# Sixteen more items of a top-k attention turned by VectorE squares and a round trip through DRAM, on one core

## The chip, the cores and the metric

The kernel runs on one core of one Trainium2 chip. The metric is the device time of one execution in microseconds (us). The kernel before was run three times: 1480.83 us is the median, 1480.33 and 1480.93 us are the ends.

## The reference

Two blocks follow each other, all in float32. First comes attention that keeps only the 32 largest scores of each query:

```
B, H, S, D = 8, 8, 576, 64
scores = scale * np.matmul(q, k.transpose(0, 1, 3, 2))
kth = np.partition(scores, -32, axis=-1)[..., -32:-31]
scores = np.where(scores >= kth, scores, -1e9)
attn = softmax(scores, axis=-1)
x = np.matmul(attn, v)            # to (B*S, H*D) = (4608, 512)
```

Then an MLP with the exact GELU:

```
h = x @ w_in                      # 512 -> 2048
out = gelu(h) @ w_out             # 2048 -> 512
```

## The kernel before

**Items and slots.** Two heads make a pair, and 128 query rows of a pair make an item; the last 64 rows of four heads make an item of their own kind. A batch has 18 items (16 main, 2 of the last rows), the eight batches have 144. Everything is done in a written-out order of slots, one for each item (the loop `for n in range(ahead)`). Two batches, 36 slots, make a round, and everything repeats from round to round. An item is called here by its place in the round, its number modulo 36 (`i % RINGS`).

**What a slot holds.** An item passes through several slots. Slot n makes the scores of item n + 2 on TensorE, and in an even slot those of item n + 3 too (`scores`); an ACT copy brings each from PSUM into one of six SBUF buffers named `s`. The keys are 512 (main) and 64 (the end of each head); the products with the end keys are made apart (`last_keys`). VectorE then looks for the 32 largest of item n by four rounds of MAX8 and MATCH_REPLACE8 (`top_k`); before them stand the larger halves of item n + 1 (`larger`) and, in some slots, transposes that lay out q and k of a later pair (`squares` in `transpose_qk`). At the end of `top_k` the callback `last` takes the reciprocal of the sums of item n - 1 (`inverse`, L504), which GpSimd has finished in `add_small` (tile `den`, L510), and which come from the exponentials of item n - 1 on ScalarE (`softmax`, L529). GpSimd then makes the threshold of item n (`threshold`, L497 and L498, which `select` on ScalarE waits for), normalises item n - 1 (`normalise`, L552), and adds up halves for item n + 2 (`sum_up`).

**How the attention weights are turned.** The product with v needs the normalised weights with the keys on the partitions. There are two ways:

- Items that are not "squared": in slot i + 2 TensorE makes nine 128x128 transposes (`tails`, L619, and `both`, L649), and ScalarE copies them from PSUM into the tile `pt` (L629, L664).
- Items for which `squared(i)` is true, which are even ones only: in slot i + 2 VectorE transposes all 32x32 squares of the item's buffer in place (`square_p`, the callback `middle` of `top_k`, L569, ahead of the third round); four DMAs write it to DRAM (`write_p`, L579); in slot i + 3 four DMAs read it back with the squares in their new places (`read_p`, L586). All are issued from SyncE's queue, in the order in which the program has them.

An even and an odd item share a `pt` tile, of which there is one. In slot i + 3 of the odd item the product with v is made for both (`attend`, L715), right after the scores, and copied to `xT`, from which the MLP takes its tokens.

**The MLP's pieces.** The MLP is cut into pieces, and each slot issues some of them between its other work; `room_in(n)` says how many. Several PSUM tiles are shared: the first of two scores of an even slot and the MLP's `h_ps` take turns in one tile.

**Loads.** From batch 1 on, q and k of a pair are loaded by eight DMAs each (L124): four for the 512 main rows and four for the 64 end rows of two heads and two halves of their 64 columns.

Of the kernel before, what the change touches and what calls it, by code (L numbers as in the profile page):

```python
# [8 lines left out]
TOPK = 32  # L9
# [5 lines left out]
def kernel(  # L15
# [26 lines left out]
    P = 128  # L42
# [68 lines left out]
    def load(n, pair, queue=None, queue2=None):  # L111
        if pair >= n_pairs:
            return
        queue = queue or nc.sync
        queue2 = queue2 or queue
        b, h0 = pair // NP, 2 * (pair % NP)
        src = sources[n]
        if n != "v" and pair >= SQUARES:
            t = flat[n][0]
            for e in range(2):  # L120
                for d in range(2):
                    rows, cols = slice((2 * e + d) * SQ, (2 * e + d + 1) * SQ), slice(d * SQ, (d + 1) * SQ)
                    for at, lo, hi, by in ((0, 0, SM, queue), (SM + e * TL, SM, S, queue2)):
                        by.dma_start(  # L124
                            out=t[rows, at : at + hi - lo].rearrange("i (c j) -> i c j", j=SQ),
                            in_=src[b, h0 + e, lo:hi, cols].rearrange("(c i) j -> i c j", i=SQ),
                        )
            return
        t = raw_of(n, pair)
        for e in range(2):  # L130
            queue.dma_start(
                out=t[:, 0:NM, e, :], in_=src[b, h0 + e, 0:SM].rearrange("(t p) d -> p t d", p=P)
            )
            queue2.dma_start(out=t[e * TL : (e + 1) * TL, NM, e, :], in_=src[b, h0 + e, SM:S])
# [141 lines left out]
    def transpose_qk(pair, first=False):  # L276
# [4 lines left out]
        def squares(c):  # L281
            rq, rk, kt = flat["q"][0], flat["k"][0], kt_of.get(pair)
            if c == 0:
                nc.vector.transpose(kt[:, 0:q_tail], rk)
            elif c == 1:
                nc.vector.transpose(kt[:, q_tail:], rq[:, SM:])
            else:
                nc.vector.transpose(q_of[pair], rq[:, 0:SM])
# [15 lines left out]
        def piece(c):  # L304
            if c == 0:
                kt_of[pair] = work.tile([P, 2 * P + SM], f32, tag="kt", bufs=NP + 2, name="kt")
            if c == 2:
                q_of[pair] = work.tile([P, SM], f32, tag="qm", bufs=NP, name="qm")
            (squares if pair >= SQUARES else by_pe)(c)
            done.add(c)  # L310
            ahead = 1 if pair >= SQUARES else 2
            if pair + ahead >= SQUARES > pair:
                return
            if c != 0 and done >= {1, 2}:
                load("q", pair + ahead)
            if (c == 0 if pair >= SQUARES else c != 0 and done >= {0, 1, 2}):
                load("k", pair + ahead)
# [5 lines left out]
    S_of, stat_of = {}, {}  # L323

# [19 lines left out]
    def last_keys(i, t_ps):  # L344
# [3 lines left out]
        if t < NM:  # L348
            nc.tensor.matmul(
                t_ps[:, 0:P], lhsT=q_of[pair][:, t * P : (t + 1) * P],  # L350
                rhs=kt_of[pair][:, SM : SM + P], start=True, stop=True,
# [8 lines left out]
        for r in range(2):  # L360
            kt = kt_of[pair + r]
            for e in range(2):
                nc.tensor.matmul(
                    t_ps[half(r, e), r * TL : (r + 1) * TL],
                    lhsT=kt[:, SM + P + e * TL : SM + P + (e + 1) * TL],
                    rhs=kt[:, SM + e * TL : SM + (e + 1) * TL],
                    start=True, stop=True,
                )
# [5 lines left out]
    def scores(i, second=False):  # L374
# [7 lines left out]
        if t < NM:  # L382
            q_t, kt = q_of[pair][:, t * P : (t + 1) * P], kt_of[pair]
            for e in range(2):
                rows = slice(e * D, (e + 1) * D)
                nc.tensor.matmul(  # L386
                    s_ps[:, e], lhsT=q_t[rows, :], rhs=kt[rows, 0:SM], start=True, stop=True
# [7 lines left out]
        else:  # L395

            for r in range(2):
                kt = kt_of[pair + r]
                for e in range(2):
                    rows = slice(e * D, (e + 1) * D)  # L400
                    nc.tensor.matmul(
                        s_ps[half(r, e), r, :], lhsT=kt[rows, SM + P + e * TL : SM + P + (e + 1) * TL],
                        rhs=kt[rows, 0:SM], start=True, stop=True,
# [53 lines left out]
    def top_k(i, last, middle):  # L457
# [21 lines left out]
        for r, (src, dst, x) in enumerate(rounds):  # L479
            if 16 * r == TOPK:  # L480
                middle()
            for e in range(2):
                nc.vector.max(x[:, e], src[:, e])  # L483
# [96 lines left out]

    def read_p(i):

        if squared(i):
            d = turned.pop(i)
            for k in range(P // SQ):
                nc.sync.dma_start(  # L586
                    out=pt_now[0][k * SQ : (k + 1) * SQ, :, 0:P], in_=d[:, :, k, :]
                )

    def transposes(i):  # L590
# [3 lines left out]
        if squared(i):  # L594

            def keys_only(ahead):
                pt_now[0] = work.tile([P, 2 * NM + 1, 2 * P], f32, tag="pt", bufs=1, name="pt")
# [7 lines left out]
        def tails(ahead):  # L605
# [3 lines left out]
            if t % 2 == 0:  # L609
                pt_now[0] = work.tile([P, 2 * NM + 1, 2 * P], f32, tag="pt", bufs=1, name="pt")  # L610
# [480 lines left out]
    def room_in(n):  # L1091
# [6 lines left out]
        return sizes[x] + (1 if x % 2 == 0 else -1)  # L1098
# [55 lines left out]
    for n in range(ahead):  # L1154
# [23 lines left out]
        product = attend(n - 3)  # L1178
# [71 lines left out]
        run_gelus()  # L1250
        if n < N:
            top_k(n, lambda: inverse(n - 1), lambda: square_p(n - 2))
# [26 lines left out]
        if n == 5:  # L1279
            load("q", SQUARES)  # L1280
# [39 lines left out]
```

## Time and profile before

| | |
|---|---|
| median of three runs | 1480.83 us |
| the profiled execution | 1479.73 us |
| its span | 1478.0 us |
| instructions | 27006 |
| TensorE busy (PE) | 1461.6 us, 99% |
| weight loads (PEld) | 1147.9 us, 78% |
| VectorE (DVE) | 1294.3 us, 88% |
| GpSimd (POOL) | 1140.1 us, 77% |
| ScalarE (ACT) | 1099.9 us, 74% |
| DMA | 112.94 MB, of 16 engines' time 35.3% in SyncE's queue |

An engine's busy time is the time in which one of its instructions runs, waits left out. Rows of the timeline begin with the start and the duration in us, then the engine and the line of the kernel. "SPq" is SyncE's queue as it issues DMAs; such a row's duration is that of the issuing, not of the transfer. A wait is shown in brackets with what ended it. Two records of TensorE stand for each float32 matmul, one for each transpose. A bracket `x8` says that eight records are merged in the row.

### The profile page before, as it was taken

The numbers are of one execution on the slowest core, as the hardware profiler recorded it, in microseconds if no ns is written. First come the engines' busy times: TensorE is split into PE (matmuls) and PEld (weight loads), VectorE is DVE, ScalarE is ACT, GpSimd is POOL, SyncE is SP. The second block draws the span as 40 slices with busy tenths as digits, with TensorE's granted clock in tenths as the row PEclk, the third lists the DMA queues.
The fourth block names the chain that finished last, engine by engine and source line by source line (L and its number), as shares of the span: only waits on it lengthen the run. The fifth ranks groups of instructions, "written<-read, shape, count | busy, mean of one in ns | idle before, by whom it ended". The sixth has DMA issues, their size and how long they took to land. (4 is left out here: it accounts for less than half of the span.)

```text
span 1478.0 us, 27006 instructions
## 1 busy us (share of the span) xinstructions
PE 1461.6 (99%) x8817; PEld 1147.9 (78%) x8817; DVE 1294.3 (88%) x3318; ACT 1099.9 (74%) x1942; POOL 1140.1 (77%) x1291
## 2 busy tenths in 40 slices
PE   8999999999999999999999999999999999999999
PEld 6876677877777777887777778787777777787787
DVE  8999899999999988999999987999999997998701
ACT  7999977877777687777777778777777777776620
POOL 6877567877898879877898978886788887987732
PEclk9999999999999999999999999999999999999999
DMA  7424310045435322345534331345453421233300
GB/s 198 143 86 124 84 48 1 24 88 101 95 73 93 66 58 52 65 95 108 105 83 81 69 61 47 66 93 99 97 103 73 89 55 41 61 61 72 70 15 15
DMA packets 477645, 112.94 MB, mean 76 GB/s; under 512 B 413216, under 2 KB 469056, under 8 KB 477504
## 3 DMA queue, kind: packets, MB, share of 16 engines
q1 hardware_dynamic: 476240, 110.78, 35.3%
q8 instruction: 70, 1.15, 0.3%
q14 instruction: 71, 0.58, 0.1%
q10 hardware_dynamic: 1200, 0.39, 0.1%
q0 software_dynamic: 64, 0.03, 0.0%
HBM read 73.39 MB, written 37.75 MB: 75 GB/s over the span
## 5 line engine op out<-in xcount | busy, mean ns | idle before, releaser
L773 PE MATMUL h_ps<-xT,w_in_sb 128*128 128x256 f32 (+1 forms) x2560 | 536.2, 361 | 0.1
L773 PEld LDWEIGHTS h_ps<-xT,w_in_sb 128*128 128x128 f32 x2560 | 436.5, 190 | 73.4 <-issue 25.2
L483 DVE MAX8 top<-lists 128x8 f32<-128x576 f32 (+1 forms) x792 | 476.4, 641 | 0.0
L486 DVE MATCH_REPLACE8 lists<-top,lists 128x288 f32<-128x288 f32 (+1 forms) x528 | 307.9, 589 | 0.0
L552 POOL TENSOR_TENSOR s<-s,rden 128x1152 f32<-128x1152 f32 x135 | 285.8, 2117 | 0.3 <-DVE rden L504 0.3
L529 ACT ACTIVATE s<-s,bias 128x576 f32<-128x576 f32 x288 | 225.4, 787 | 11.0 <-issue 0.4
L517 ACT ACTIVATE s<-s,neg 128x576 f32<-128x576 f32 x288 | 225.5, 793 | 1.7 <-POOL neg L497 1.6
L510 POOL TENSOR_SCALAR den<-den 128x2 f32<-128x2 f32 x144 | 31.4, 218 | 215.9 <-ACT s L529 210.2
L455 POOL TENSOR_TENSOR lists<-lists 128x576 int32<-128x576 int32 x132 | 186.2, 1410 | 4.0
L447 POOL TENSOR_TENSOR lists<-s 128x576 int32<-128x576 int32 x133 | 187.2, 1407 | 0.0
L715 PE MATMUL o<-pt,raw_v 128*64 128x256 f32 x1280 | 153.0, 384 | 1.8 <-ACT s L529 1.1
L715 PEld LDWEIGHTS o<-pt,raw_v 128*64 128x64 f32 x1280 | 87.8, 136 | 85.8 <-issue 37.2
L789 ACT ACTIVATE g<-h_ps 128x512 f32<-128x512 f32 x144 | 78.2, 594 | 100.6 <-PE h_ps L773 100.4
L929 PE MATMUL y_ps<-w_out_sb,sum 128*128 128x256 f32 x472 | 140.4, 379 | 0.0
L394 ACT ACTIVATE s<-s_ps 128x1024 f32<-128x1024 f32 x127 | 125.5, 1035 | 10.5 <-PE s_ps L386 10.3
L664 ACT COPY pt<-tp 128x1024 f32<-128x1024 f32 x85 | 86.6, 1019 | 62.2 <-PE tp L649 62.1
L386 PE MATMUL s_ps<-kt,qm 64*128 64x512 f32 x512 | 129.4, 618 | 0.8 <-ACT s L392 0.8
L504 DVE RECIPROCAL rden<-den 128x2 f32<-128x2 f32 x144 | 23.2, 161 | 108.6 <-POOL den L510 107.4
L486 DVE MATCH_REPLACE8 lists<-first,lists 128x288 f32<-128x288 f32 x264 | 114.3, 439 | 0.0
L929 PE MATMUL y_ps<-w_out_sb,g 128*128 128x256 f32 x480 | 113.4, 379 | 0.0
L483 DVE MAX8 first<-lists 128x8 f32<-128x288 f32 x268 | 106.6, 436 | 0.0
L929 PEld LDWEIGHTS y_ps<-w_out_sb,g 128*128 128x128 f32 x480 | 91.2, 190 | 12.4
(167 smaller groups left out, 2533.1 us busy)
## 6 DMA issues: line engine op xcount, KB each, us to landing
turned<-s SPq DMA_DIRECT2D x192, 144.0 KB, 3.5
pt<-turned SPq DMA_DIRECT2D x192, 144.0 KB, 3.2
raw_v<-in_v_dram SPq DMA_DIRECT2D x64, 128.0 KB, 2.4
out_dram<-y SPq DMA_DIRECT2D x30, 256.0 KB, 2.1
raw_q<-in_q_dram SPq DMA_DIRECT2D x112, 64.0 KB, 2.0
raw_k<-in_k_dram SPq DMA_DIRECT2D x112, 64.0 KB, 2.0
w_out_sb<-in_moe_w_in_dram SPq DMA_DIRECT2D x14, 511.8 KB, 4.8
w_out_sb<-in_moe_w_out_dram SPq DMA_DIRECT2D x10, 511.8 KB, 4.1
```

What stands on the lines that cost most here:

```text
L386: nc.tensor.matmul(s_ps[:, e], lhsT=q_t[rows, :], rhs=kt[rows, 0:SM], start=True, stop=True)
L394: nc.scalar.activation(spread(s, S + TL, SM), s_ps, func=AF.Copy, scale=scale)
L447: nc.gpsimd.tensor_tensor(t[:, :, 1].bitcast(i32), a.bitcast(i32), b.bitcast(i32), op=ALU.add)
L455: nc.gpsimd.tensor_tensor(into_of(i)[:, :, 1].bitcast(i32), both, top, op=ALU.subtract)
L483: nc.vector.max(x[:, e], src[:, e])
L486: nc.vector.match_replace(dst[:, e], x[:, e], src[:, e], LOWEST)
L517: nc.scalar.activation(s, s, func=AF.Prelu, bias=st["neg"][:, e : e + 1], scale=1.0, alpha=STEEP)
L529: nc.scalar.activation(s, s, func=AF.Exp, bias=st["bias"][:, e : e + 1], scale=1.0, accum_out=st["den"][:, e : e + 1],)
L552: nc.gpsimd.tensor_tensor(s, s, wide, op=ALU.mult)
L715: nc.tensor.matmul(o[e * D : (e + 1) * D, 0:n], lhsT=vt[:, j, e, :], rhs=pt[:, e * NJ + j if j < NM else NM, :], start=(j == 0), stop=(j = ...
L773: nc.tensor.matmul(h_tile(u)[:, i, :], lhsT=w_in_sb[:, ko, f * P : (f + 1) * P], rhs=xT[:, ko, c0 : c0 + n], start=(ko == 0), stop=(ko == ...
L929: nc.tensor.matmul(acc[names][:, k], lhsT=lhsT, rhs=rhs, start=(j == 0 and k == 0), stop=(j == FT // 2 - 1 and k == 1),)
```

## The change

Sixteen odd items (places 3, 13, 21, 25 and 29 of a round, from item 29 on) are squared too. For such an item i, which `later(i)` tells:

- the nine transposes on TensorE and their ACT copies go; VectorE squares, four writes and four reads come;
- in slot i + 1 the reciprocal is taken between the last two MAX8 instead of behind them (`early`), and normalising comes ahead of the next item's threshold on GpSimd;
- in slot i + 2 the squares are made behind the first round of `top_k` instead of ahead of the third (`late`), and the writes come as soon as they are done; loads that the slot issues come after them;
- in slot i + 3 the product with v moves from the slot's beginning to its end, and two MLP pieces move from slot i + 2 to slot i + 3 (`moved`).

Beside that, q and k of all pairs from batch 1 on are loaded by four DMAs each instead of eight. For it the first head's 64 end keys are taken from the beginning of its rows and its main keys from behind them, v's rows are loaded in the same order, the end keys of a pair lie at both ends of its tile (`both_ends`), and the transpose that lays out q's end rows is 64 instead of 128 columns wide.

```diff
             for e in range(2):
+                at = e * TL if n == "k" else 0
                 for d in range(2):
...
-                    for at, lo, hi, by in ((0, 0, SM, queue), (SM + e * TL, SM, S, queue2)):
-                        by.dma_start(
-                            out=t[rows, at : at + hi - lo].rearrange("i (c j) -> i c j", j=SQ),
-                            in_=src[b, h0 + e, lo:hi, cols].rearrange("(c i) j -> i c j", i=SQ),
-                        )
+                    queue.dma_start(
+                        out=t[rows, at : at + S].rearrange("i (c j) -> i c j", j=SQ),
+                        in_=src[b, h0 + e, :, cols].rearrange("(c i) j -> i c j", i=SQ),
+                    )
...
-                nc.vector.transpose(kt[:, q_tail:], rq[:, SM:])
+                nc.vector.transpose(kt[:, q_tail : q_tail + TL], rq[:, SM:S])
...
             if c != 0 and done >= {1, 2}:
-                load("q", pair + ahead)
+                issue(lambda: load("q", pair + ahead))
             if (c == 0 if pair >= SQUARES else c != 0 and done >= {0, 1, 2}):
-                load("k", pair + ahead)
+                issue(lambda: load("k", pair + ahead))
...
+    def both_ends(pair):
+        kt = kt_of[pair]
+        return spread(kt, SM + TL, TL) if pair >= SQUARES else kt[:, SM : SM + P]
...
-    def top_k(i, last, middle):
+    def top_k(i, last, middle, early, late):
...
-            if 16 * r == TOPK:
+            if 16 * r == TOPK and not late:
                 middle()
             for e in range(2):
                 nc.vector.max(x[:, e], src[:, e])
+                if early and e == 0 and r == len(rounds) - 1:
+                    last()
+            if r == 0 and late:
+                middle()
...
-            if r == len(rounds) - 1:
+            if r == len(rounds) - 1 and not early:
                 last()
...
     def squared(i):
-        return SINGLE.stop - 2 < i < N - 2 and i % 2 == 0 and items[i][1] < NM and i % RINGS != 12
+        if not SINGLE.stop - 2 < i < N - 2 or items[i][1] == NM:
+            return False
+        if i % 2 == 0:
+            return i % RINGS != 12
+        return i % RINGS in LATER
+    def later(i):
+        return i % 2 == 1 and squared(i)
     RINGS = 2 * len(items) // B
+    LATER = (3, 13, 21, 25, 29)
...
                 nc.sync.dma_start(
-                    out=pt_now[0][k * SQ : (k + 1) * SQ, :, 0:P], in_=d[:, :, k, :]
+                    out=pt_now[0][k * SQ : (k + 1) * SQ, :, i % 2 * P : (i % 2 + 1) * P], in_=d[:, :, k, :]
                 )
...
-        return sizes[x] + (1 if x % 2 == 0 else -1)
+        moved = 2 * (later(n - 3) - later(n - 2))
+        return sizes[x] + (1 if x % 2 == 0 else -1) + moved
...
-        product = attend(n - 3)
+        product = not later(n - 3) and attend(n - 3)
...
         run_gelus()
         mlp(left[0])
         run_gelus()
+        if later(n - 3):
+            attend(n - 3)
+            copy_x()
         if n < N:
-            top_k(n, lambda: inverse(n - 1), lambda: square_p(n - 2))
+            top_k(
+                n, lambda: inverse(n - 1), lambda: square_p(n - 2), later(n - 1), later(n - 2)
+            )
             write_p(n - 2)
             flush()
...
+        if later(n - 1):
+            normalise(n - 1)
         threshold(n)
...
-        normalise(n - 1)
+        if not later(n - 1):
+            normalise(n - 1)
         sum_up(n + 2)
```

More of the change, by code (lines that the diff above doesn't have):

```diff
@@ L130, in load @@
         for e in range(2):
+            end = TL if pair >= SQUARES and e == 0 else S
+            main = end % S
             queue.dma_start(
-                out=t[:, 0:NM, e, :], in_=src[b, h0 + e, 0:SM].rearrange("(t p) d -> p t d", p=P)
+                out=t[:, 0:NM, e, :], in_=src[b, h0 + e, main : main + SM].rearrange("(t p) d -> p t d", p=P)
             )
-            queue2.dma_start(out=t[e * TL : (e + 1) * TL, NM, e, :], in_=src[b, h0 + e, SM:S])
+            queue2.dma_start(out=t[e * TL : (e + 1) * TL, NM, e, :], in_=src[b, h0 + e, end - TL : end])
     load("k", 0, nc.scalar, nc.gpsimd)
@@ L350, in last_keys @@
                 t_ps[:, 0:P], lhsT=q_of[pair][:, t * P : (t + 1) * P],
-                rhs=kt_of[pair][:, SM : SM + P], start=True, stop=True,
+                rhs=both_ends(pair), start=True, stop=True,
             )
@@ L386, in scores @@
                 nc.tensor.matmul(
-                    s_ps[:, e], lhsT=q_t[rows, :], rhs=kt[rows, 0:SM], start=True, stop=True
+                    s_ps[:, e], lhsT=q_t[rows, :], rhs=kt[rows, main_keys(pair)], start=True, stop=True
                 )
@@ L401, in scores @@
                     nc.tensor.matmul(
-                        s_ps[half(r, e), r, :], lhsT=kt[rows, SM + P + e * TL : SM + P + (e + 1) * TL],
-                        rhs=kt[rows, 0:SM], start=True, stop=True,
+                        s_ps[half(r, e), r, :], lhsT=kt[rows, end_rows(pair + r, e)],
+                        rhs=kt[rows, main_keys(pair + r)], start=True, stop=True,
                     )
@@ L579, in write_p, with pt_tile @@
                 nc.sync.dma_start(out=d[:, :, rows], in_=s[rows])
+    def pt_tile():
+        return work.tile([P, 2 * NM + 1, 2 * P], f32, tag="pt", bufs=1, name="pt")
     def read_p(i):
@@ L1279 @@
         if n == 5:
+            nc.vector.memset(flat["k"][0][TL:, 0:TL], 0.0)
             load("q", SQUARES)
```

16 lines of the change are left out of this document (12 added, 4 removed).

## The prediction

> **What bounds the kernel now.** I read the page's first part, then a table of three whole rounds of 36 slots, then who waited for whom, then the timeline of the slots that the change touches.
>
> ```profile
> PE 1461.6 (99%) x8817; PEld 1147.9 (78%) x8817; DVE 1294.3 (88%) x3318; ACT 1099.9 (74%) x1942; POOL 1140.1 (77%) x1291
> 355.57:703.63 348.06, 347.65 (x2085) 273.79 (x2083) 321.89 (x833) 262.71 (x470) 286.34 (x323) 1.00 0.40 79
> DVE rden L504 <- POOL den L510: 107.4, 92, 9.7
> ```
>
> TensorE is busy without a break: 347.65 of 348.06 us of a round, 9.67 us a slot. So what it no longer has to do is time won, as long as nothing else is late. Little is spare elsewhere: VectorE works 321.89 us of the round and idles 26.2, nearly all of it at the reciprocal, where it waits for `den` (107.4 us in all).
>
> **TensorE's saving.** One item's transposes, between neighbours in the order:
>
> ```profile
> 1331.42 0.60 PE L891 MATMUL y_ps<-w_out_sb,g 128*128 128x256 f32 x2
> ...
> 1335.10 0.27 PE L619 MATMUL tp_t<-ident,s 128*128 128x128 f32 x1
> 1335.21 0.60 PE L891 MATMUL y_ps<-w_out_sb,g 128*128 128x256 f32 x2
> ...
> 1336.07 1.04 PE L649 MATMUL tp<-ident,s 128*128 128x128 f32 x8
> 1336.94 0.38 PE L891 MATMUL y_ps<-w_out_sb,g 128*128 128x256 f32 x1
> ```
>
> The tail's transpose takes TensorE 1335.21 - 1335.10 = 0.11 us, the eight others 1336.94 - 1336.07 = 0.87 (ends are modelled, so starts count). Sixteen items by 0.98 make 15.7 us, 1.06% of the time. The ACT copies that go with them lie on an engine that is busy 74% and are worth nothing by themselves. The tail behind the last product has the same four MLP blocks in the new order, so nothing is pushed out to the end.
>
> **VectorE.** A square takes 1.36 us (next fence), so 16 add 21.8 us, 6.8 to a round that has 26.2 idle. On average that fits; it is local slots that decide. The narrower layout of q's end rows (0.27 us now) may save up to half of that on 28 transposes, 3.8 us at most and nothing at least; I take 2, hidden in the same idle time. The one new memset is 64x64, below the 0.27 us row in size, and hidden.
>
> **The way over DRAM, on item 129 (place 21).** Its even partner 128 shows what the way costs:
>
> ```profile
> 1269.56 1.36 DVE L569 STREAM_TRANSPOSE s<-s 128x1152 f32<-128x1152 f32 x1
> 1273.60 1.40 DVE L483 MAX8 top<-lists 128x8 f32<-128x576 f32 x2
> 1275.04 0.76 DVE L422 TENSOR_TENSOR lists<-s 128x576 f32<-128x576 f32 x1
> 1275.71 0.81 DVE L483 MAX8 first<-lists 128x8 f32<-128x288 f32 x2
> 1274.30 0.22 POOL L510 TENSOR_SCALAR den<-den 128x2 f32<-128x2 f32 x1
> 1275.99 2.10 POOL L552 TENSOR_TENSOR s<-s,rden 128x1152 f32<-128x1152 f32 x1
> 1270.99 3.38 SPq L579 DMA_DIRECT2D turned<-s  x4
> 1277.10 2.55 SPq L586 DMA_DIRECT2D pt<-turned  x4
> DMA to landing us min/median/max: 2.7/3.3/5.2
> 1283.79 2.38 PE L715 MATMUL o<-pt,raw_v 128*64 128x256 f32 x20
> 1286.10 2.86 PE L773 MATMUL h_ps<-xT,w_in_sb 128*128 128x256 f32 x12
> 1289.01 4.48 PE L773 MATMUL h_ps<-xT,w_in_sb 128*128 128x256 f32 x20
> 1293.33 1.03 PE L927 MATMUL seven<-w_sum,g 128*128 128x256 f32 x4
> ```
>
> From the first write's issue (1270.99) to the first read's (1277.10), which waits for the writes to land, pass 6.1 us; the fourth read goes out 1.9 us later and lands 3.3 us behind its issue (the median). So `pt` is full 11.3 us after the writes begin.
>
> When do the writes of 129 begin? `den` of 129 is ready at 1274.52. The reciprocal now goes between the two last MAX8 (the pair begins at 1273.60, 0.67 us each), at about 1274.55, and normalising, 2.10 us, ends at 1276.85 instead of 1278.09. VectorE does the second MAX8 (0.70), `larger` (0.68) and the first round (0.75), is at the square by 1276.85 too, and is through at 1278.25. But SyncE's queue issues the reads of 128 until 1277.10 + 2.55 = 1279.65, so the writes begin then and `pt` is full at 1290.95.
>
> When does TensorE want it? The product (1286.10 - 1283.79 = 2.31 us) now stands near the slot's end, ahead of two of the four-record MLP steps (20 records take 1293.33 - 1289.01 = 4.32, so 4 take 0.86) and of 1293.33. On an engine that won 0.98 it begins at 1293.33 - 0.86 - 2.31 - 0.98 = 1289.2. It waits 1.75 us there: this item costs 0.8 instead of winning 0.98. The two moved MLP pieces only fill the place that the product left.
>
> **The other four places, by the same steps.**
>
> ```profile
> 1098.24 0.17 DVE L504 RECIPROCAL rden<-den 128x2 f32<-128x2 f32 x1 [1.09 <-POOL den L510]
> 1099.29 2.54 SPq L586 DMA_DIRECT2D pt<-turned  x4
> 1116.71 1.03 PE L927 MATMUL seven<-w_sum,g 128*128 128x256 f32 x4
> 1120.90 0.33 PE L619 MATMUL tp_t<-ident,s 128*128 128x128 f32 x1 [0.35 <-POOL s L552]
> ```
>
> Place 3 (item 111). `den` gates the reciprocal (1.09 us of waiting with both MAX8 done), so it stays at 1098.24; normalised at 1100.55, squared at 1101.95, the reads of 110 are out at 1101.83. `pt` is full at 1113.3, wanted at 1116.71 - 0.86 - 2.31 - 0.98 = 1112.55: 0.7 us of waiting, which would leave 0.3 won. But in the next slot but one TensorE stands at item 113's tail for its normalising (0.35 us), and that chain is not shortened: GpSimd, full here, now normalises before it makes the threshold, and what it did while the reciprocal ran it does behind it, some 0.2 us (the reciprocal's 0.17 and a start). So place 3 costs 0.2.
>
> ```profile
> 1193.21 0.17 DVE L504 RECIPROCAL rden<-den 128x2 f32<-128x2 f32 x1 [0.21 <-POOL den L510]
> 1193.97 0.83 DVE L284 STREAM_TRANSPOSE kt<-raw_k 128x640 f32<-128x640 f32 x1
> 1194.73 0.27 DVE L286 STREAM_TRANSPOSE kt<-raw_q 128x128 f32<-128x128 f32 x1
> 1194.83 3.87 SPq L124 DMA_DIRECT2D raw_k<-in_k_dram  x8
> 1211.92 1.09 PE L401 MATMUL s_ps<-kt 64*64 64x512 f32 x8
> ```
>
> Place 13 (item 121). The reciprocal stays at 1193.21; VectorE passes the second MAX8 (0.70), `larger`, the two layouts above and the first round, and has squared at 1197.8. Behind its writes, ahead of its reads, the order puts k's and q's loads, eight DMAs now: the row has eight in 3.87 us. Writes 3.4, loads 3.9: the reads begin at 1205.1, later than the landing would let them (1203.95). `pt` is full at 1210.3, wanted at 1211.92 - 2.31 - 0.98 = 1208.6. It waits 1.7 and costs 0.7.
>
> ```profile
> 1311.57 0.17 DVE L504 RECIPROCAL rden<-den 128x2 f32<-128x2 f32 x1 [0.24 <-POOL den L510]
> 1313.50 2.55 SPq L586 DMA_DIRECT2D pt<-turned  x4
> 1321.06 0.17 DVE L504 RECIPROCAL rden<-den 128x2 f32<-128x2 f32 x1 [1.40 <-POOL den L510]
> 1332.19 2.10 POOL L552 TENSOR_TENSOR s<-s,rden 128x1152 f32<-128x1152 f32 x1
> ```
>
> Place 25 (item 133). Squared by 1315.3, the reads of 132 are out at 1316.05, `pt` is full at 1327.35, wanted at 1331.42 - 0.90 - 2.31 - 0.98 = 1327.2. That would do. But VectorE has to make up a MAX8 (0.70) behind the wait and a square (1.30 beyond its overlap) where it had 1.40 us of waiting: its next reciprocal comes 0.6 later than 1321.06. GpSimd's slot behind it is full, and item 135 is normalised at 1334.9 instead of 1334.29. TensorE would want it 0.98 ahead of its 1335.10 and waits 0.8. Won: 0.2.
>
> ```profile
> 1000.75 1.42 DVE L483 MAX8 top<-lists 128x8 f32<-128x576 f32 x2
> 999.95 0.22 POOL L510 TENSOR_SCALAR den<-den 128x2 f32<-128x2 f32 x1 [1.93 <-ACT s L529]
> 1004.11 2.54 SPq L586 DMA_DIRECT2D pt<-turned  x4
> 1022.67 1.03 PE L927 MATMUL seven<-w_sum,g 128*128 128x256 f32 x4
> ```
>
> Place 29 (item 101). `den` was ready at 1000.17, so the reciprocal moves up to 1001.42, the square ends at 1005.1, the reads of 100 are out at 1006.65, `pt` is full at 1017.95 and wanted at 1022.67 - 0.86 - 2.31 - 0.98 = 1018.5. Nothing waits: 0.98 won.
>
> **The loads.** A DMA of q or k takes SyncE's queue 0.48 us whatever its size (3.87 / 8), so half as many save 1.9 us of issuing a load, on a queue that nobody waits for in the slots without squares; they buy the room between writes and reads. I cost them at nothing; place 13 has them in its sum.
>
> **Two rules.** The row for transposes is above: 0.98 us of TensorE against 1.36 of VectorE, 5.9 us of issuing and 11.3 us of way. The Trainium skill (VectorE: DVE Perf Modes, Rules for kernel authors) says to turn 128x128 on TensorE where the result may lie in PSUM, or by the DMA's own transposer, and not by a strided plain copy; by it the change would lose. If all sixteen fared as place 21, it would be 16 x 0.8 = 13 us slower. In the other direction, TensorE's row says 99%. The Trainium skill (Perfetto Trace Analysis, Identifying the Most-Contended Engine) says to relieve the most contended engine first, and that matmul busy time is a poor measure of it, to be replaced by the share of weight loads, here 78%. By the first half of that the whole 15.7 us would be won.
>
> **The sum.** Place 29 comes four times: -3.9. Places 25, 21, 13 and 3 come three times: -0.6, +2.4, +2.1, +0.6. Together +0.6 us. Two additions: writes that go out while reads are landing, or next to loads, land later than alone. The slowest landed after 5.2 us, the median after 3.3; I take 0.45 of those 1.9 us, at places 21 and 13: 6 x 0.45 = 2.7. And VectorE comes 0.6 us late out of place 25 into place 29, where slots without waiting follow; I take 0.3 in each of three rounds, 0.9. Total +4.2: 1479.73 + 4.2 = 1483.9 for a profiled execution, and as the median of the runs shown lies 1.1 above it, 1485.0.
>
> **The rivals.**
> 1. *The full way is won.* If the landings are hidden after all (`pt` full two us earlier at places 3, 13 and 21, because the writes need not queue behind the reads, or because TensorE is late there for other reasons), only the chains of places 3 and 25 are left: 4 + 3 + 3 places at 0.98 win 9.8, place 25 0.6, place 3 costs 0.6: 9.8 us faster, 1471; with those chains shortened too, 1465. For it speaks that 0.7 to 1.75 us decide, and that TensorE waits for nothing now; against it, that the queue's order is fixed and that 6.1 us between write and read repeat. It holds from 1.7 us of earlier landing on. 0.34.
> 2. *DMA becomes the bound of the pairs.* Where write, read, write, read follow each other slot by slot, each way lands as late as the slowest does now, 1.9 us more. Then place 21 costs 2.7, 13 2.6, 3 1.6, 25 1.1 and 29 0.3: 3 x 8.0 + 1.2 = 25 us slower, 1506. For it: odd items put a second pair of transfers into a slot. Against: the engines are 40% busy in these rounds (the table's DMA share). 0.14.
> 3. My sum, costs and gains near cancelling: 0.52.
>
> **The numbers.** Less than 0.2%, 3 us, cannot be told from no change here. The likeliest is my sum: 1485.0, with its own range 1480 (no additions, and 2 us from VectorE's narrower transposes) to 1491. Of its 0.52, 0.13 falls within 3 us of now and 0.39 above; rival 1 is faster, rival 2 slower. So faster 0.34, same 0.13, slower 0.53. The range for 8 in 10 takes in rival 1 as worked out but not its last step, and the lower half of rival 2: 1469 to 1497.
>
> **What the profile after would show.** Right: TensorE's busy time lower by about 16 us, its idle time higher by as much or more; waits of the product with v (`o`) for a DMA into `pt`, of 1 to 2 us, at places 13 and 21 and none at 29; the normalising of items 5 and 27 still just ahead of their tails. VectorE about 20 us busier, its wait for `den` well under 107 us. Wrong: no waits of `o` for DMA (then rival 1, and I placed the writes too late); waits of 3 us and more at every place (rival 2); or ACT standing for the writes ahead of its copies of the scores, since the buffer of a squared odd item goes to the item six later in slot i + 3: by my times it would stand until 1285.8 at place 21 and still be in time.

## The result, and the profile after

The changed kernel takes 1523.80 us (median of 4 runs, 1520.12 to 1527.04) against 1480.88: 1.029 times as long, 95% interval 1.0264 to 1.0316. The prediction said 1485.0, within 1469 to 1497. The direction was the likelier one; the size lies far outside, beyond even the rival in which DMA binds (1506).

First the busy times, then the group of `larger`, then who waited for whom (total in us, times, longest), all of the changed kernel. The last two rows are of the kernel before:

```profile
PE 1456.6 (96%) x8673; PEld 1137.4 (75%) x8673; DVE 1335.6 (88%) x3335; ACT 1081.3 (71%) x1910; POOL 1143.4 (75%) x1291
...
L443 DVE TENSOR_TENSOR lists<-s 128x576 f32<-128x576 f32 x133 | 122.8, 924 | 0.6
...
POOL neg L522 <- DVE rden L529: 73.5, 48, 3.6
ACT s L415 <- DMA turned<-s: 34.1, 11, 4.5
ACT s L542 <- POOL neg L522: 27.0, 17, 3.9
PE o L753 <- DMA pt<-turned: 33.2, 18, 4.7
PE h_ps L811 <- ACT s L415: 4.7, 8, 0.7
PE tp_t L657 <- POOL s L577: 4.0, 6, 1.2
...
L422 DVE TENSOR_TENSOR lists<-s 128x576 f32<-128x576 f32 x133 | 100.8, 758 | 0.0
ACT s L517 <- POOL neg L497: 1.6, 6, 0.4
```

TensorE was 99% busy and is 96%: its idle time rose from 16.4 us (1478.0 - 1461.6) to 61.7 (1518.3 - 1456.6), by 45.3. Of these, 29.5 are stands of the product at fourteen of the sixteen new items, 7.7 stands of the product at other pairs, 4.7 stands at `h_ps`, and 2.9 come on top at the tails.

Its busy time fell by 5.0 and not by 16. The transposes are gone as reckoned: counted from start to start, without the stands, the transposes and the products with the end keys beside them take 16.4 us less. But all other matmuls together take 11.4 us more. Some 3 us of these are the ends of records: TensorE stands 50 times where it stood 18 times (stands over 0.15 us), and ahead of a stand the last matmul shows its full length of 0.38 us, where otherwise 0.22 or 0.31 pass until the next one starts. Some 5 us are a slower TensorE after the three longest stands, at place 13 (last section). The rest, some 3 us, was not followed up. Together 45.3 + 11.4 - 16.4 = 40.3, what the span grew by.

VectorE got 41.3 us busier (1294.3 to 1335.6). The squares account for 21.8 of that; another 22.0 are the row of `larger` (L443): 122.8 us, where the kernel before had 100.8 for the same 133 instructions (L422). The narrower layouts of q's end rows give 1.8 back.

The slot of item 129, which the prediction followed, on all engines (VectorE, GpSimd, SyncE's queue, ScalarE, TensorE). The last two rows are the two reciprocals of the same slot in the kernel before:

```profile
1312.11 0.17 DVE L529 RECIPROCAL rden<-den 128x2 f32<-128x2 f32 x1 [0.22 <-POOL den L535]
1312.96 2.11 DVE L443 TENSOR_TENSOR lists<-s 128x576 f32<-128x576 f32 x1
1315.73 1.36 DVE L603 STREAM_TRANSPOSE s<-s 128x1152 f32<-128x1152 f32 x1
...
1323.52 0.14 DVE L529 RECIPROCAL rden<-den 128x2 f32<-128x2 f32 x1
1312.36 2.11 POOL L577 TENSOR_TENSOR s<-s,rden 128x1152 f32<-128x1152 f32 x1 [0.28 <-DVE rden L529]
1314.43 0.72 POOL L522 TENSOR_SCALAR neg<-top 128x2 f32<-128x2 f32 x1
1314.65 2.55 SPq L625 DMA_DIRECT2D pt<-turned  x4
1317.30 3.32 SPq L613 DMA_DIRECT2D turned<-s  x4
1324.55 2.54 SPq L625 DMA_DIRECT2D pt<-turned  x4
1315.19 0.78 ACT L542 ACTIVATE s<-s,neg 128x576 f32<-128x576 f32 x1 [1.97 <-POOL neg L522]
1319.83 1.00 ACT L415 ACTIVATE s<-s_ps 128x1024 f32<-128x1024 f32 x1
1324.73 1.03 ACT L415 ACTIVATE s<-s_ps 128x1024 f32<-128x1024 f32 x1 [3.90 <-DMA turned<-s]
1327.29 0.26 ACT L379 ACTIVATE s<-t_ps 128x128 f32<-128x128 f32 x1
1320.89 1.13 PE L811 MATMUL h_ps<-xT,w_in_sb 128*128 128x256 f32 x4 [0.67 <-ACT s L415]
1329.72 2.38 PE L753 MATMUL o<-pt,raw_v 128*64 128x256 f32 x20 [2.30 <-DMA pt<-turned]
...
1274.93 0.14 DVE L504 RECIPROCAL rden<-den 128x2 f32<-128x2 f32 x1
1283.17 0.17 DVE L504 RECIPROCAL rden<-den 128x2 f32<-128x2 f32 x1
```

Five things are to be seen.
- `larger` (1312.96) lies beside the normalising that was moved ahead (GpSimd, 1312.36 to 1314.47). It takes 2.11 us instead of 0.76 and ends 0.6 us behind it, as if it had run only once GpSimd was through. So the square ends at 1317.09, 4.98 us behind the reciprocal. The prediction had 3.7.
- VectorE goes from this reciprocal to the next (1323.52) without a gap, in 11.41 us. In the kernel before the same slot took 8.24 (1283.17 - 1274.93).
- The writes (1317.30) go out 0.21 us behind the square and 0.10 behind the partner's four reads (1314.65 + 2.55 = 1317.20), which stand ahead of them on the queue. The odd item's own reads follow 7.25 us after the writes, and TensorE stands 2.30 us for them.
- ScalarE's second copy of the scores (1324.73) stands 3.90 us until those writes have landed, for it fills the buffer that they read. The copy of the keys' rows (1327.29) comes behind it. That copy empties the one PSUM bank which the product, too, writes. Here it was in time: the product waited longer, for its reads.
- `h_ps` stood 0.67 us for the first of the two copies (1319.83). That one did not stand for the writes. It came late because ScalarE had stood 1.97 us for `neg`, GpSimd's threshold, which comes behind the normalising that was moved ahead. In the trace each of the eight stands of `h_ps` follows such a stand of ScalarE, of 0.5 to 2.0 us. In all, ScalarE stands 27.0 us for `neg`; before, it was 1.6.

### The profile page after: what moved, and what is told of

Read it like the earlier page. It is cut to its first block, busy times and chain, and to the rows that moved or that the text cites. A ratio compares the mean times of both kernels' runs of the same rounds, so it can differ in the third digit from the quotient of the medians.

```text
span 1518.3 us, 26593 instructions
## 1 busy us (share of the span) xinstructions
PE 1456.6 (96%) x8673; PEld 1137.4 (75%) x8673; DVE 1335.6 (88%) x3335; ACT 1081.3 (71%) x1910; POOL 1143.4 (75%) x1291
## 5 line engine op out<-in xcount | busy, mean ns | idle before, releaser
L753 PE MATMUL o<-pt,raw_v 128*64 128x256 f32 x1280 | 157.2, 391 | 39.0 <-DMA pt<-turned 33.2
L753 PEld LDWEIGHTS o<-pt,raw_v 128*64 128x64 f32 x1280 | 94.4, 139 | 113.4 <-issue 51.7
L522 POOL TENSOR_SCALAR neg<-top 128x2 f32<-128x2 f32 x144 | 74.0, 514 | 83.2 <-DVE rden L529 73.5
L443 DVE TENSOR_TENSOR lists<-s 128x576 f32<-128x576 f32 x133 | 122.8, 924 | 0.6
L529 DVE RECIPROCAL rden<-den 128x2 f32<-128x2 f32 x144 | 22.8, 158 | 100.8 <-POOL den L535 100.1
```

The lines of the kernel that those rows point to most:

```text
L753: nc.tensor.matmul(o[e * D : (e + 1) * D, 0:n], lhsT=vt[:, j, e, :], rhs=pt[:, e * NJ + j if j < NM else NM, :], start=(j == 0), stop=(j = ...
```

## The experiments

Ratios are against the kernel before, run beside it on the same chip. The first result of each heading is the median.

**The loads alone: 1488.49 us, ratio 1.0057 (1.0040 to 1.0073).**

```diff
-    LATER = (3, 13, 21, 25, 29)
+    LATER = ()
```

> No odd item is squared (the list of places is empty); the four-DMA loads of q and k, their order behind the writes and the narrower layouts stay. Theory A (the loads cost nothing, all 43 us come with the odd items): 1479 to 1481, and no stand of the product with v for its DMAs. Rival L (the loads, held until a slot's writes are out, also delay the reads of the next even item): the 6.7 us that TensorE lost in the changed kernel at the products of items 31, 35, 37, 47, 67, 71, 103 and 107, none of which is a new item, stay, and the time is about 1487.

Rival L is right: the loads cost 8 us with no odd item changed. SyncE's queue in this kernel, and one of the six stands (1.1 to 1.7 us) of the product of items 31 and 35 of a round:

```profile
672.21 3.35 SPq L613 DMA_DIRECT2D turned<-s  x4
675.61 2.88 SPq L124 DMA_DIRECT2D raw_k<-in_k_dram  x4
678.58 0.44 SPq L134 DMA_DIRECT2D raw_v<-in_v_dram  x1
...
682.21 2.59 SPq L625 DMA_DIRECT2D pt<-turned  x4
687.62 2.38 PE L753 MATMUL o<-pt,raw_v 128*64 128x256 f32 x20 [1.12 <-DMA pt<-turned]
```

k's four DMAs, now held until the writes are out, stand with v's between the writes (672.21) and the reads (682.21): 10.0 us from one to the other, where 6.1 do without loads.

**The same loads, not held: 1479.99, ratio 0.9996 (0.9987 to 1.0006). The loads behind the reads: 1480.49, ratio 1.0000 (0.9991 to 1.0009).**

```diff
-                issue(lambda: load("q", pair + ahead))
+                load("q", pair + ahead)
...
```
```diff
-        held[0] = n < N and squared(n - 2)
         read_p(n - 3)
+        flush()
+        held[0] = n < N and squared(n - 2)
...
             write_p(n - 2)
-            flush()
+            held[0] = False
```

Both have `LATER = ()` as well.

> As the kernel with the loads alone (no odd item over DRAM, 1488.5), but k and q are loaded as soon as their layouts are done, as before the change, and not behind the writes of the slot. Theory H (the hold is what costs: the loads stand on SyncE's queue between the writes and the reads of the items 30 and 34 of a round, and TensorE stands 1.2 to 1.8 us at each of those two products): the stands are gone, 1479 to 1481. Rival (four large DMAs in place of eight land later or fill the engines, wherever they go out): 1486 to 1489.

> As the kernel with the loads alone, but what is held goes out behind the reads of the item (k, q and v), not between its writes and its reads. Theory H: the two stands of a round go, 1479 to 1482, unless v, k or q then come late, which would show as stands for raw_k or raw_v. Rival (traffic, not the order): 1486 to 1489.

Theory H in both: the time is the old one. Four DMAs for eight are worth nothing either way; the place on the queue is worth 8 us.

**ScalarE normalises the odd items: 1502.55, ratio 1.0152 (1.0137 to 1.0167).**

```diff
         s, r = S_of[i].rearrange("p (e n) -> p e n", e=2), stat_of[i]["rden"]
...
+        if later(i):
+            for e in range(2):
+                nc.scalar.activation(row(i, e), row(i, e), func=AF.Copy, scale=r[:, e : e + 1])
+            return
```

> The changed kernel, but the 16 odd items are normalised by ScalarE (two copies with the reciprocal as scale) and not by GpSimd. Theory P (VectorE's 'larger' and GpSimd's normalising shut each other out: larger takes 2.11 us where the two lie side by side, 0.76 elsewhere, so that the square ends 1.35 us late): larger is back at 0.76 in all slots, the square ends 3.4 to 3.7 us behind the reciprocal instead of 4.97, TensorE's stands at the product shrink by 1.3 us each (17 us in all, more where ScalarE's stands shrink too): 1496 to 1507. Rival W (the way through DRAM is simply too long wherever it starts, larger is slow for another reason, such as its data coming late): larger stays near 2 us, 1521 to 1527.

```profile
L443 DVE TENSOR_TENSOR lists<-s 128x576 f32<-128x576 f32 x133 | 101.1, 761 | 0.6
POOL neg L522 <- DVE rden L529: 39.1, 40, 3.1
PE o L757 <- DMA pt<-turned: 13.8, 11, 2.6
```

Theory P by its time, 21.3 us less: `larger` is back at 101.1 us, the squares end 3.6 us behind the reciprocal (4.5 at place 13), and the product's stands for its reads fall from 33.2 to 13.8 us. They do not all fall in the way that the theory has it. At place 21 the writes leave as late as before, 5.1 us behind the reciprocal, with the last of the partner's reads, and the early square only waits there. Its product's stands shrink (4.7 to 0.5 us over its three items), but 1.1 us at each item now lie ahead of it, at the keys' rows, where TensorE waits for copies by ScalarE. GpSimd's threshold (`neg`), no longer behind 2.1 us of normalising, gains as well (ScalarE's stands for it fall from 27.0 to 3.4 us); the run does not part the two.

**Nothing moved forward: 1525.09, ratio 1.0305 (1.0284 to 1.0325).**

```diff
-                n, lambda: inverse(n - 1), lambda: square_p(n - 2), later(n - 1), later(n - 2)
+                n, lambda: inverse(n - 1), lambda: square_p(n - 2), False, False
...
-        if later(n - 1):
-            normalise(n - 1)
         threshold(n)
...
-        if not later(n - 1):
-            normalise(n - 1)
+        normalise(n - 1)
```

> The changed kernel, but nothing moved forward: reciprocal behind the last MAX8, normalising behind the threshold, square and writes at the place that even items have. The product stays at the slot's end. Theory P (the early normalising takes back on VectorE, 1.35 us at larger, and at the threshold, 2.1 us later, what it wins for the writes): larger at 0.76 everywhere, 1510 to 1522. Rival W (only the start of the writes counts, some 0.7 us later than in the changed kernel): stands at the product 0.7 us longer in 16 places, 1530 to 1540.

```profile
L443 DVE TENSOR_TENSOR lists<-s 128x576 f32<-128x576 f32 x133 | 101.1, 761 | 0.0
PE o L753 <- DMA pt<-turned: 39.4, 16, 5.0
```

Between the two expectations, and in neither: `larger` is back at 101.1 us, but the square comes 5.3 us behind the reciprocal, and the product's stands grow to 39.4. In exchange `h_ps` and the tails hardly wait, and ScalarE's stands for `neg` are 5.8 us in place of 27.0. Moving the steps forward bought nothing: what it won for the writes it lost at `larger` and behind `neg`.

**Scores put off, with GpSimd normalising: 1538.09, ratio 1.0385 (1.0370 to 1.0401); with ScalarE: 1516.21, ratio 1.0245 (1.0229 to 1.0260).**

```diff
-        two = few[0] and n % 2 == 0 and n + 3 < N and items[n + 3][1] < NM
+        two = few[0] and n % 2 == 0 and n + 3 < N and items[n + 3][1] < NM and not later(n - 3)
```

> The changed kernel, but in the slot in which an odd item's writes are still under way the second pair of scores is put off to the next slot, so that ScalarE's copy of it does not stand for the buffer that those writes still read. Theory B (this stand costs: h_ps for ScalarE's copy 6.25 us, and part of the 5 us at the tails behind it): the stand of the copy of the scores for the DMA of the writes (34 us of ScalarE) is gone, 1513 to 1518. Rival (the stand lies beside other work, as the prediction had it): 1522 to 1526.

> ScalarE normalises the odd items, and the second pair of scores is put off by a slot as well, so that no copy stands for the buffer of the writes. Theory B (with VectorE and GpSimd relieved, the stand of the copy is what is late: 7.9 us at h_ps and 9 at the keys' rows behind it): 1488 to 1496. Rival V (VectorE's chain sets these slots, and TensorE only waits at another place, as in the kernel with the scores put off alone): 1500 to 1512.

Both missed; each is 14 us above the kernel that it changes. `h_ps` no longer stands, for it no longer takes turns with these scores in one PSUM tile (both expectations put its stand down to the landing of the writes, wrongly, as the slot of item 129 shows). But the scores that are put off now come behind the product in TensorE's order: they wait with it, ScalarE's copy of them comes late, and the reciprocal two slots on later still (from reciprocal to reciprocal 11.61 us at place 23, 8.04 in the changed kernel). The edit moves a wait to where VectorE is late; it says nothing for or against ScalarE's stand.

**Place 29 alone: 1490.94, ratio 1.0068 (1.0053 to 1.0083).** The edit is `LATER = (29,)`.

> Only the four items of place 29 go over DRAM; all else as changed. Theory A with the stands as the changed kernel's trace has them (1.97, 1.95, 1.56 and 0 us at the product, 0.98 won per item, about 0.25 us more for each stand): 1.5 to 3 us above the kernel with the loads alone. If the stands of place 29 were made by the places before it (VectorE or the queue late from them), place 29 alone wins its 0.98 each: 3 to 4 us below the kernel with the loads alone.

2.5 us above the loads alone, theory A. Its product stands 1.6 and 1.7 us at two of its four items, with no other place changed: these stands are not made by the other places. One cause of them, q's held loads, is told under the prediction's errors, below.

**The product freed of the odd item's way: 1526.73, ratio 1.0318 (1.0302 to 1.0333); and without the odd squares: 1506.97, ratio 1.0186 (1.0169 to 1.0203).**

```diff
-            if i % 2 == 0:
-                pt_now[0] = pt_tile()
-            for k in range(P // SQ):
...
+            if i % 2 and squared(i - 1):
+                return
...
+            for x in (1,) if i % 2 else range(1 + squared(i + 1)):
+                for k in range(P // SQ):
...
```
and, for the second, `if squared(i) and not later(i):` ahead of the square.

> The changed kernel, but for the 13 odd items outside place 13 the half of pt comes from the even partner's matrix in DRAM, and its reads go out with the partner's (the odd item's own writes still go out, and nobody reads them; the output of these items is not the reference's). So the product no longer depends on the square, the writes and their landing, while VectorE, GpSimd, ScalarE and the queue do the same work. Theory W (what loses is the way): the stands at those products go, about 20 us with what follows each: 1497 to 1503. Theory V (VectorE's slots with an odd square, 11.4 us in one piece, set the pace): TensorE only stands elsewhere, at the tails or behind ScalarE: 1508 to 1520.

> As the kernel with the partner's reads, and the odd items' squares on VectorE are left out too (their matrices are written to DRAM as they are). Theory W: nothing more is won, within 3 us of the kernel with the partner's reads. Theory V: 16 squares of 1.36 us off a VectorE that sets the pace, 10 to 20 us below it.

The first gained nothing at all, against both theories, and the trace tells why:

```profile
956.38 5.16 SPq L628 DMA_DIRECT2D pt<-turned  x8
961.66 3.69 SPq L613 DMA_DIRECT2D turned<-s  x4
968.05 1.03 ACT L415 ACTIVATE s<-s_ps 128x1024 f32<-128x1024 f32 x1 [5.33 <-DMA turned<-s]
970.60 0.26 ACT L379 ACTIVATE s<-t_ps 128x128 f32<-128x128 f32 x1
970.91 2.38 PE L756 MATMUL o<-pt,raw_v 128*64 128x256 f32 x20 [1.61 <-ACT s L379]
```

Eight reads in one go keep the queue until 961.54; the writes of item 93 go out 2.6 us later than four reads would let them. ScalarE's copy stands 5.33 us for their landing, the keys' rows come behind it, and the product stands for the PSUM bank. So there are two ways through the same landing, by `pt` and by ScalarE, and cutting one shows the other. The second, 20 us faster, has the size of theory V, but without the squares its writes also go out earlier; it can't part the two. The kernels without those writes, below, come nearer to it.

**Both causes taken away: loads behind the reads, ScalarE normalising: 1525.35, ratio 1.0306 (1.0290 to 1.0321); place 29 alone so: 1491.31, ratio 1.0073 (1.0058 to 1.0088).** The edits are the two shown above.

> Two causes taken away together: ScalarE normalises the odd items, and what is held goes out behind the reads. All 16 items. If the causes add up: 1502.6 - 8.0 = 1494 to 1495, and lower where place 13's loads no longer stand between its writes and reads (2.3 us in 3 places): 1487 to 1495. If the late loads now hold VectorE's layouts up: 1496 to 1502.

> The same with place 29 alone (4 items, ideally 3.9 us). Its stands at the product with ScalarE normalising were 1.9, 0.8, 0.3 and 0 us. If they go with the loads out of the way: 1477 to 1478.5. If VectorE's extra 1.36 us a slot takes back what TensorE saves: 1480 to 1482.

Both missed. Loads behind the reads of an even item now stand ahead of the odd partner's writes; in the second kernel:

```profile
661.17 2.54 SPq L629 DMA_DIRECT2D pt<-turned  x4
663.75 2.23 SPq L124 DMA_DIRECT2D raw_q<-in_q_dram  x4
666.08 3.36 SPq L617 DMA_DIRECT2D turned<-s  x4
672.04 2.63 SPq L629 DMA_DIRECT2D pt<-turned  x4
677.73 2.38 PE L757 MATMUL o<-pt,raw_v 128*64 128x256 f32 x20 [2.00 <-ACT s L554]
```

q's loads (663.75) put the writes of item 65 back to 666.08, and the product stands 2.00 us. (The row puts that down to ScalarE, but by the trace the fourth read lands at 677.29, and the copy that empties the PSUM bank had ended at 675.70.) What was free with even squares only is not with pairs.

**The loads not held, ScalarE normalising: 1496.48, ratio 1.0106 (1.0091 to 1.0121).**

> All 16 odd items, normalised by ScalarE, and k and q loaded as soon as their layouts are done, as before the change (v is held as ever). If the two causes add up: 1502.6 - 8.0 = 1494.6, 1491 to 1497. If SyncE's early loads now delay the writes: 1498 to 1503.

Here the causes add up, 6.1 us of the 8.

**The same kernels without the odd items' writes: GpSimd normalising 1497.40, ratio 1.0116 (1.0101 to 1.0131); ScalarE 1485.05, ratio 1.0029 (1.0017 to 1.0041).**

```diff
-        if squared(i):
+        if later(i):
+            S_of.pop(i)
+        elif squared(i):
...
-            d = turned.pop(i)
+            d = last_d[0] if i % 2 else turned.pop(i)
+            last_d[0] = d
```

> The changed kernel with k's and q's loads not held, and the odd items are squared on VectorE but not written to DRAM: their half of pt is read from an even item's matrix that has long landed, at the same place of SyncE's queue (their output is not the reference's). So neither the product nor ScalarE's copies hang on the landing of an odd item's writes. Theory W (both ways through the landing are what loses): TensorE's stands go, 1480.0 - 15.7 = 1464, up to 1470. Theory V (VectorE's slots of 11.4 us, and GpSimd's threshold behind the normalising, set the pace too): 1478 to 1500.

> As the kernel without the odd items' writes, and ScalarE normalises them. Theory W: within 4 us of the kernel without the writes, since VectorE's 1.35 us then lie beside TensorE's work. Theory V: 8 to 20 us below it.

Theory V by the times, in both. With GpSimd normalising, hardly anything waits for a landing any more, and TensorE still loses the whole saving and 17 us. Its waits in the first kernel, and one of them with what it waited for:

```profile
PE tp_t L660 <- POOL s L577: 21.5, 16, 1.9
956.39 0.17 DVE L529 RECIPROCAL rden<-den 128x2 f32<-128x2 f32 x1 [0.42 <-POOL den L535]
957.24 2.10 POOL L577 TENSOR_TENSOR s<-s,rden 128x1152 f32<-128x1152 f32 x1
959.40 0.33 PE L660 MATMUL tp_t<-ident,s 128*128 128x128 f32 x1 [1.86 <-POOL s L577]
```

Fifteen of the 16 stands at tails, all but 0.2 us of the 21.5, are at the item two behind an odd square. The sixteenth (item 141) stands in the kernel before as well. The search of that item lies in the slot with the odd square, where VectorE has 11.4 us (12.3 at place 13), so its reciprocal comes late, its normalising late with it, and TensorE's tail waits. In nine of the fifteen VectorE does not idle ahead of that reciprocal; in six, as in the one shown, it also waits 0.4 or 1.1 us for `den`, which hangs on the same search by way of the threshold and the exponentials. With ScalarE normalising the slot has 10.04 us (10.4 at place 25, 10.9 at 13), and these stands are gone. As above, that edit relieves GpSimd too, so VectorE's share is argued from the order of the rows, not parted from GpSimd's. What TensorE still loses more than before, counted from start to start, is 8 us ahead of `h_ps` and 9 ahead of the keys' rows, each for a copy by ScalarE, which had stood for the reciprocal ahead of its normalising:

```profile
ACT s L578 <- DVE rden L529: 31.4, 16, 2.9
```

**Place 29 alone, the loads not held, ScalarE normalising: 1479.17, ratio 0.9994 (0.9984 to 1.0004).**

> Place 29 alone (4 items) with ScalarE normalising and the loads not held: what is left to win at the place that the prediction had as the best. All of it: 1480.0 - 3.9 = 1476. If its stands stay (1.9, 0.8, 0.3 and 0 us with all places): 1478 to 1480.5.

The best of all kernels here, and not to be told from the kernel before.

## Why the prediction was wrong

The step that failed is what the sixteen ways cost the engines beside TensorE. The working had 12.5 us of stands at the products of the new items (15.2 with its addition for late landings), late normalising at the tails of places 3 and 25 alone, and the loads at nothing. Measured were 29.5 us at these products, 7.7 at others, 4.7 at `h_ps`, and 5 us of a slower TensorE. Three terms lie behind that: `larger` at its old duration, the loads, and the work that waits behind VectorE's longer slots and behind GpSimd's threshold.

| place | stand of the product predicted, us | measured | what came later than predicted |
|---|---|---|---|
| 29 | 0 | 1.9, 1.9, 1.5, 0 | the partner's reads, behind q's held loads |
| 3 | 0.7 | 1.7, 2.3, 1.8 | the square, by 1.3; the way, by 0.6 to 1.1 |
| 13 | 1.7 | 3.8, 4.7, 4.2 | the square, by 1.2; the way, by 1.3 to 1.8 |
| 21 | 1.75 | 1.2, 1.2, 2.3 | at the third item the way, by 1.0 |
| 25 | 0 | 0.4, 0, 0.6 | the writes, by 0.6 to 1.0 |

Each of these stands ends 0.14 to 0.23 us after the last read has landed. At place 29, the best place by the prediction, three of the four items have q's held loads ahead of their partner's reads. This is item 101 in the changed kernel, whose partner's reads wait behind q's loads:

```profile
1030.64 3.00 SPq L124 DMA_DIRECT2D raw_q<-in_q_dram  x4
1033.82 2.55 SPq L625 DMA_DIRECT2D pt<-turned  x4
1036.48 3.59 SPq L613 DMA_DIRECT2D turned<-s  x4
```

From the partner's writes (1026.76) to its reads pass 7.1 us in place of 6.0 before the change, and item 101's writes leave 6.45 us behind the reciprocal, where the prediction had 5.2. The first three items of place 29 have such loads, and stand. The fourth has none: its partner's reads leave after 6.1 us, and its product does not stand. In the last kernel above, with loads not held, the four stand 1.3, 0.3, 0 and 0 us: at the first something else adds, which was not followed up.

- *TensorE's saving*: right. 16.4 us are gone, where 15.7 were predicted. That its busy time would fall by as much was wrong, for the reasons told above.
- *The square at 1278.25*: wrong, by 1.2 to 1.3 us at all sixteen items. The step added `larger` at the duration that it had in the trace of before, 0.68, though it had just put GpSimd's normalising beside it. It took 2.11. The Trainium skill states the rule that was missed (SBUF — State Buffer, Who interferes with whom): VectorE with two inputs in SBUF and a GpSimd instruction that reads SBUF share one port as an exclusive lock, and whichever comes second waits until the first is through. The traces agree: 2.11 us beside GpSimd, 0.76 when ScalarE does the same work. This set the start of the writes at eight items only (places 3 and 13, two of place 25). At the other eight the partner's reads were the last to go, and the writes went out 0.10 to 0.13 us behind them. At place 21 that was 5.2 us behind the reciprocal, where the prediction had 5.1: there its start of the writes was right, and its stand about right.
- *VectorE, "on average that fits; it is local slots that decide"*: right as a sentence, wrong as applied. I followed the chain to the tail at places 3 and 25 alone and priced it at 0.2 and 0.8. The kernel without the odd items' writes shows the tail waiting behind fifteen of the sixteen, 1.4 us on average; in the changed kernel, where the product stands as well, 4.0 us at six tails are left of it. 26.2 us of idle time in a round are no reserve: they lie in other slots, where VectorE waits for `den`.
- *The way*: right in the main. From the first write to a full `pt` pass 10.9 to 12.4 us outside place 13 (predicted 11.3), and 13.8 to 14.3 at place 13, where the loads lie between (12.5).
- *The loads "at nothing"*: wrong by 8 us, half of what the change could win. I looked at the loads that lie behind the sixteen writes, not at those of even items, which the same hold moves. The same hold put q's loads between the partner's writes and reads at place 29.
- *ScalarE "still in time"*: right at place 21 in the changed kernel, where its copy stood until 1324.73, and the product waited longer for its own reads. But it is a second way through the same landing, over the PSUM bank, that I did not see: it was the last wait in the kernel with the partner's reads. The order on GpSimd, normalising ahead of the threshold, I priced at 0.2 us and at place 3 alone; ScalarE's stands for `neg` and the stands of `h_ps` show that it held ScalarE up at most of the new items.
- *Rival 1* fell at its first condition, earlier landings. *Rival 2* came nearest in time, by another cause: the landings took as long as before (3.5 us for a write, 3.2 for a read, medians in both kernels). Of the two rules that were weighed, the one that keeps 128x128 transposes on TensorE had the right sign; the one that relieves the most contended engine first did not bear, for the load went to an engine with no room in those slots.

How the 43 us divide can only be told in order, since cutting one wait uncovers the next: from 1523.8, ScalarE's normalising takes away 21.3, loads not held 6.1 more, leaving out the odd writes 11.4 more. That leaves 1485.05, some 21 above the ideal of 1464; of these, 17 are the stands behind ScalarE, counted as above. How much of the 21.3 is `larger` and how much is `neg` stays open. A third list buffer, with which `larger` could go ahead of the normalising, was not tried.

## What to carry to other kernels

Idle time of the second-busiest engine is only worth what lies in the slot that gets the work: write the slot's instructions one behind the other, with each one's neighbours on the other engines, before you call it hidden. Moving an instruction forward changes what it runs beside, so its duration in the old trace no longer holds. And a queue in order has no free place between a write and the read that follows: a load put there, or ahead of the write, is paid for by whoever waits for the read, and by the write that is queued behind that read.

## What the runs showed of the hardware

After the three longest stands of the changed kernel, 3.81, 4.74 and 4.18 us at place 13, TensorE was slower for some 5 us. The timeline of TensorE at the third, and a window that has the granted clock (the third number from the right, behind the busy times of the five engines):

```profile
1245.49 3.47 PE L753 MATMUL o<-pt,raw_v 128*64 128x256 f32 x20 [4.18 <-DMA pt<-turned]
1248.88 1.63 PE L422 MATMUL s_ps<-kt 64*64 64x512 f32 x8
...
1246.64:1250.04 3.40, 3.40 (x20) 1.41 (x16) 3.40 (x8) 0.37 (x1) 0.96 (x2) 0.50 0.53 81
```

20 products took 3.47 us where 2.38 are usual, and eight scores 1.63 where 1.09 are. The granted clock was 0.50 for 3.4 us. The shorter stands of the changed kernel, up to 2.30 us, show nothing of this. The Trainium skill has the rule (TensorE: Matmul & The Clock Gate, Part 1: The HAM clock gate): after an idle window of about 3.4 us the clock falls to half. The traces agree on the half, but not on a stand of that length as its condition. In the kernel in which ScalarE normalises, this stand of 2.21 us was enough:

```profile
519.29 4.07 PE L757 MATMUL o<-pt,raw_v 128*64 128x256 f32 x20 [2.21 <-DMA pt<-turned]
519.37:522.78 3.41, 3.41 (x18) 2.34 (x20) 3.41 (x7) 0.00 (x0) 1.94 (x3) 0.50 0.35 55
```

So was one of 2.07 us in the same kernel, and one of 2.56 was not. The length of the stand alone does not decide; what does was not followed up. In the changed kernel the three long stands cost 1.6, 2.1 and 1.6 us more than themselves.
